# Pinning the issue order in the feed-forward part of a two-layer spectral and gated kernel

## The chip, the cores and the metric

The kernel runs on one core of a Trainium2 chip. The metric is the device time of one execution in microseconds (us). A core has five engines, each with a queue of its own: PE multiplies matrices (PEld is its weight load, which runs beside the matmuls), DVE (VectorE), ACT (ScalarE) and POOL (GpSimd) work element by element, and SP issues DMA transfers. They wait for one another by semaphores. PE writes into PSUM, which is divided into banks. A bank holds a 128x512 f32 tile here; POOL takes its operands from SBUF alone in this kernel.

## The reference

```python
x = A_x                                       # 1 x 2048 x 512, f32
for layer in range(2):
    n = layernorm(x)                          # over the 512 features, no weights
    x = x + irfft2(rfft2(n) * (w_r + 1j * w_i))       # over tokens and features
    n = layernorm(x)
    x = x + ((n @ w_gate) * (n @ w_up)) @ w_down      # 512 -> 1792 -> 512
...
```

The reference writes the two layers out one after the other; both use the same weights.

## The kernel before

**Stages.** `x` stays in SBUF as `xs`, 16 tiles of 128 tokens by 512 features. A layer is a spectral part and a feed-forward part. The spectral part is a forward transform of each tile (`fwd_steps`: tiles `fo`, `fe`, `tp`, `fs`, `dp`, `us`, `sp`, `E`), a middle phase (`mid_phase`) and an inverse transform of each tile (`inv_steps`: matmuls `vp`, ACT copies them to `vs[0]` and DVE makes the rest `vs[1]`, 12 matmuls `yi`, three DVE additions into `xs`, then the statistics of the next norm). The edges of the parts overlap with the feed-forward part by `weave`, which mixes a main list of steps with a side list by a cost written beside each step.

**Units.** The feed-forward part does the products by a 2x2 scheme with seven products instead of eight. `build_x` normalises two token tiles, transposes them on PE (`tq`) and makes the operand forms: `xA` (three blocks, ACT and DVE) and `xS` (four blocks of sums and differences: four POOL steps at lines 434 to 437, an ACT copy at line 440, a POOL subtraction at line 441). Every f32 operand is split in two, a rounded high part and a rest, and each product runs three matmuls (high by high, high by rest, rest by high; `mm3`, line 109), for two halves of the contraction: six matmuls a product.

`unit` does one of 14 blocks `ft` of 128 hidden features, gate and up, for two groups of 512 tokens (a full unit: eight tiles of `xs`) or two groups of 256 (half a unit: four tiles). For the first half of `xs` (`h0=0`) a layer runs four half units (blocks 0 and 1), ten full units (blocks 2 to 11) and four half units (blocks 12 and 13); for the second half (`h0=8`) it goes back through the blocks in reverse order: four half units, ten full ones, four half ones. Its steps are `p1` (PSUM tile `gx`), `p6` (`gy`), `p5` (`gw`), `p2` (into `gx` again), `p7` (`gz`), `p3` (`gv`), `p4` (into `gz` again). PSUM has one bank each for the tags x (`gx`), y (`gy`, `gz`) and w (`gw`, `gv`), three for tag a and two for tag d. ACT copies `gx` to `s1` (line 530); seven DVE steps (lines 536, 542, 551, 565, 566, 572, 573) add and multiply the products; the results are split into `h` by ACT (line 558) and POOL (line 559).

**Down products.** Each unit returns a list of down products, one for each 128 tokens of each of its two results (eight for a full unit, four for half a one), which the next unit mixes between its own products. A down product is three matmuls into a `db` bank (tag d) and a DVE addition into `xs` (line 580).

**Weights.** `load_raw` has SP fetch the raw weights of a block into `rg` (one buffer). `forms_w` makes the seven operand forms in `wt` (two buffers, even and odd blocks) from it: high parts `h...` on ACT (line 470), rests `l...` on POOL (line 473), differences `d...` in place on POOL (line 476). `down_w` does the same for the down weights (`rw`, `wd`, ACT line 491, POOL line 495). `beside` hands these steps out over the products of a unit, for the block after it (`eager` for a half unit).

**What sets the order.** The program is written in one sequence, but a scheduler decides the order in each engine's queue: it takes instructions by readiness in its own estimate and then by their written place, so an instruction that it takes to be ready may pass one that is written before it. On the chip every queue runs in the order that the scheduler left.

Of the kernel before, what the change touches and what calls it, by code (L numbers as in the profile page):

```python
# [13 lines left out]
EPS = 1e-5  # L14
# [73 lines left out]
def kernel(ctx: ExitStack, tc: tile.TileContext, x, wf, wc, wb, dfwd, dinv, tf, ti, mid, out):  # L88
# [18 lines left out]
    def mm3(o, sh, sl, mh, ml, start, stop):  # L107
        for n, (a, b) in enumerate(((sh, mh), (sh, ml), (sl, mh))):
            nc.tensor.matmul(o, a, b, start=start and n == 0, stop=stop and n == 2, skip_group_check=True)  # L109

    tt, stt = nc.vector.tensor_tensor, nc.vector.scalar_tensor_tensor
    gtt = nc.gpsimd.tensor_tensor
# [5 lines left out]
    nc.vector.memset(eps, EPS)  # L118
# [5 lines left out]
    def prep_hp(after):  # L124
        wct = wk.tile([128, 4, 2, 32], F32, name="wct", tag="tw", bufs=4)
        nc.gpsimd.tensor_copy(wct[0:1, 0, 0, 0:1], after)
        nc.sync.dma_start(wct, wc)
        for ri, col, src, op, scale in ((0, 0, 0, ALU.add, 0.5), (1, 0, 1, ALU.subtract, 0.5),
                                        (0, 1, 3, ALU.subtract, -0.5), (1, 1, 2, ALU.add, 0.5)):
            tt(hp[:, ri, :, col], wct[:, src, 0], wct[:, src, 1], op)  # L130
            nc.vector.tensor_scalar(hp[:, ri, :, col], hp[:, ri, :, col], scale, None, op0=ALU.mult)
# [19 lines left out]
    def stats(t, nm):  # L151
# [4 lines left out]
        nc.vector.bn_stats(st, xs[:, t])  # L156
        nc.vector.bn_aggr(nm["mv"][:, i], st)
# [7 lines left out]
    def rstd(nm):  # L165
# [4 lines left out]
        nc.scalar.activation(q, var, AF.Sqrt, bias=eps)  # L170
        small.extend([
            lambda: nc.vector.reciprocal(r0, q),
# [6 lines left out]
    def normed(t, nm):  # L179
        fill(9)  # L180
        xn = temp("xn", "g")
        i = nm["ts"].index(t)
        nc.vector.tensor_scalar(xn, xs[:, t], nm["mv"][:, i, 0:1], nm["r"][:, i:i + 1], op0=ALU.subtract, op1=ALU.mult)
        return xn
# [10 lines left out]
    def fwd_steps(get_dc, E, tags, gs, fs_dve):  # L195
# [4 lines left out]
        def a0(t):  # L200
# [4 lines left out]
            if i == 0:  # L205
                nc.vector.tensor_scalar(m2, nm["mv"][:, :n, 0], 2.0, None, op0=ALU.mult)
# [9 lines left out]
        def a1(t):  # L216
            s = S[t]
            tp = bank("tp", tags(t)[0])
            for i in range(4):
                src = s["fo"][:, i] if i < 2 else s["fe"][:, i - 2]  # L220
                nc.tensor.transpose(tp[:, 128 * i:128 * i + 128], src, ident)
            fs = s["fs"] = temp("fs", "f")
            if fs_dve(t):
                nc.vector.tensor_copy(fs, tp)
            else:
                nc.scalar.copy(fs, tp)

        def a2(t):
# [5 lines left out]
            for i, (n, c0) in enumerate(((256, 128), (256, 128), (128, 0), (128, 64))):  # L234
                mv = dc[:, o:o + n].rearrange("p (c k) -> p c k", c=2)
                nc.tensor.matmul(dv[:, :, c0:c0 + n // 2], fs[:, 128 * i:128 * i + 128], mv,  # L236
# [3 lines left out]
            nc.gpsimd.memset(u[64:128, :, 0:257:256], 0.0)  # L240
            i = nms[t]["ts"].index(t)
            r = nms[t]["r"][:, i:i + 1]
            for jj in range(2):
                q = slice(64 * jj, 64 * jj + 64)
                nc.scalar.mul(u[0:64, jj, 0:257], dp[q, 0:257], r[q])
                nc.scalar.mul(u[64:128, jj, 1:256], dp[q, 257:512], r[q])
                fill()

        def a3(t):
            s = S[t]  # L250
            tw, u = s["tw"], s["u"]
            for jj in range(2):
                sp = bank("sp", tags(t)[2])
                nc.tensor.matmul(sp[:, :257], tw[:, jj], u[:, jj, 0:257], start=True, stop=True)  # L254
                nc.scalar.copy(E[:, t, :, jj], sp[:, 0:257])
# [14 lines left out]
    class Filter:  # L270
# [5 lines left out]
        def load(self, n, after=None):  # L276
# [9 lines left out]
            if after is not None:  # L286
                nc.gpsimd.tensor_copy(self.at[n][0:1, 0, 0:1], after)
# [6 lines left out]
    def mid_phase(E, W):  # L294
# [3 lines left out]
        def turn(n, back):  # L298
            e = E[:, :, 16 * n:16 * n + 16].rearrange("p t k j -> p k t j")
            t = T[:, 16 * n:16 * n + 16].rearrange("p k (t j) -> p k t j", j=2)  # L300
            nc.vector.transpose(*((e, t) if back else (t, e)))

        def times_w(z, jz, w, p):
            nc.scalar.mul(jz[0:64], z[64:128], -1.0)
            nc.scalar.copy(jz[64:128], z[0:64])
# [3 lines left out]
        def spec(n):  # L309
            zp = bank("zp", XYW[n % 3])  # L310
            z = zp.rearrange("p (k g) -> p k g", g=32)
            nc.tensor.matmul(z, f2, T[:, 16 * n:16 * n + 16], start=True, stop=True)
# [15 lines left out]
        def unspec(n, y):  # L328
            yp = bank("yp", "a")
            y3 = yp.rearrange("p (k g) -> p k g", g=32)  # L330
            for i, m in enumerate(y):
                nc.tensor.matmul(y3, g2, m, start=i == 0, stop=i == len(y) - 1)
            nc.scalar.copy(T[:, 16 * n:16 * n + 16], y3)
# [5 lines left out]
        for i in range(20):  # L339
# [10 lines left out]
            if i == 0:  # L350
                nc.vector.transpose(tx[:, 0].rearrange("p (t j) -> p t j", j=2), E[:, :, 256])
                xp = bank("xp", "d")
                nc.tensor.matmul(xp[:, :32], f2, tx[:, 0], start=True, stop=True)
# [8 lines left out]
    def inv_steps(E, get_dc, nms, order, tags, build):  # L362
# [5 lines left out]
        def b1(t):  # L368
# [4 lines left out]
            for par in range(2):  # L373
                for jj in range(2):
                    nc.tensor.matmul(v4[:, par, :, jj], E[:, t, 128 * par:128 * par + 128, jj],
# [3 lines left out]
            nc.scalar.copy(vs[0], vp)  # L379
# [30 lines left out]
    def build_x(X, nm, tags):  # L410
# [9 lines left out]
        def turn(h):  # L420
            tq = bank("tq", tags[h])
            xn = s["xn"][h]
            for i in range(4):
                nc.tensor.transpose(tq[:, 128 * i:128 * i + 128], xn[:, 128 * i:128 * i + 128], ident)
            s[h] = tq.rearrange("p (b k s) -> p b k s", b=2, k=2)

        def forms():
            a, b = s[0], s[1]
            S = wk.tile([128, 4, 2, 128], F32, name="sx", tag="sx")
            nc.scalar.copy(S[:, 2:4], a)  # L430
            nc.scalar.copy(S[:, 0:2], b)
            nc.scalar.copy(XA[:, 0:2, 0, :, cols], a)
            nc.scalar.copy(XA[:, 2, 0, :, cols], b[:, 1])
# [313 lines left out]
```

## Time and profile before

| what | value |
|---|---|
| three runs | 1321.7, 1324.8, 1331.17 us; median 1324.8 us |
| the profiled execution's own time | 1329.39 us |
| its span, from the first to the last instruction | 1327.6 us |
| mean granted TensorE clock | 0.957 |
| layer 0, feed-forward part in the trace | about 142 to 696 us |
| layer 1, feed-forward part in the trace | about 790 to 1320 us |
| down products | 448, of three matmuls each |
| DVE waits for `db` on PE | 110.8 us in 151 waits |
| ACT waits for PE before the `wd` copy (line 491) | 199.8 us in 42 waits |

A profile is of one execution. A line names the place in the program, the engine and the tiles (out<-in). A wait is put down to what ended last before the waiting instruction began. A matmul's own duration overlaps with the next one's, so PE's pace is read from the starts. In the trace the start of line 572's addition marks the end of each unit: in layer 1 these lie at 801.9, 812.7, 831.6 and 839.5 us for the first four half units, at 858.6 to 1032.0 us for the ten full ones, at 1047.5 and 1055.2 us for the pair of half units after them, at 1063.6 to 1123.0 us for six more half units, at 1138.1, 1158.0, 1173.5 and so on to 1282.7 us for the ten full ones of the second half, and at 1295.5 to 1319.1 us for the last four.

### The profile page before, as it was taken

What the parts mean: (1) busy time and instruction counts of PE and PEld (TensorE: products, weight loads), DVE (VectorE), ACT (ScalarE), POOL (GpSimd) and SP (SyncE); (2) the same over time, 40 slices, a digit from 0 to 9 for tenths busy, and PEclk for the clock granted to TensorE, in tenths of its full rate; (3) what the DMA queues carried; (4) which work ended last, traced back from release to release, by engine and by line L of the source; (5) the groups of instructions that cost most, each with busy time, mean ns of one, the idle gap of its engine ahead of it and who ended that gap; (6) DMA issues with size and microseconds to landing.
All of it is one profiled execution on the core that took longest, in us unless ns stands there. A gap on an engine that the chain in (4) does not pass through costs nothing.

```text
span 1327.6 us, 16468 instructions
## 1 busy us (share of the span) xinstructions
PE 1188.2 (89%) x5804; PEld 958.1 (72%) x5804; DVE 896.1 (67%) x1669; ACT 460.9 (35%) x931; POOL 755.6 (57%) x788
## 2 busy tenths in 40 slices
PE   5888789989888889999998978999989878899998
PEld 4736678868667777788785467787776777677777
DVE  8578747768567866765685975586765655566666
ACT  5875323222222343344336732322212232322221
POOL 3543457565563676766622534766556465777772
PEclk9999889989999899999998988998999988999999
DMA  5541001112010011111105310111121021111111
GB/s 220 195 146 41 24 20 56 56 33 88 32 32 9 9 41 48 52 57 53 39 19 218 112 32 17 48 57 40 32 64 32 33 72 38 51 48 48 32 33 64
DMA packets 30754, 77.67 MB, mean 59 GB/s; under 512 B 3408, under 2 KB 11856, under 8 KB 28368
## 3 DMA queue, kind: packets, MB, share of 16 engines
q1 hardware_dynamic: 29952, 73.54, 16.8%
q0 software_dynamic: 288, 2.10, 0.5%
q8 instruction: 46, 0.75, 0.2%
q10 hardware_dynamic: 432, 0.98, 0.2%
q14 instruction: 36, 0.29, 0.1%
HBM read 72.42 MB, written 4.19 MB: 58 GB/s over the span
## 4 chain that ended last, share of the span: by engine, by line
PE 60%; POOL 20%; DVE 6%; issue 5%; ACT 5%; DMA 2%; POOLq 0%; ACTq 0%; SPq 0%; DVEq 0%
PE db L109 21%; PE gz L109 10%; PE gx L109 7%; POOL rg L476 5%; POOL wt L473 5%; PE gv L109 5%; PE gw L109 4%; POOL h L559 4%; PE gy L109 3%; PE yi L109 3%; PE dp L236 2%; PE sp L254 2%; POOL jz L307 2%; POOL xS L441 2%; DMA rg<-in_wb_dram 2%
## 5 line engine op out<-in xcount | busy, mean ns | idle before, releaser
L109 PE MATMUL db<-wd,h 128*128 128x512 f32 x1344 | 390.2, 412 | 56.1 <-POOL h L559 37.6
L580 DVE TENSOR_TENSOR xs<-xs,db 128x512 f32<-128x512 f32 x448 | 304.2, 684 | 112.2 <-PE db L109 110.8
L109 PEld LDWEIGHTS db<-wd,h 128*128 128x128 f32 x1344 | 246.9, 194 | 132.1 <-POOL h L559 56.5
L473 POOL TENSOR_TENSOR wt<-rg,wt 128x256 fp32r<-128x256 f32 x200 | 233.6, 1175 | 87.9 <-ACT wt L470 80.4
L470 ACT CAST wt<-rg 128x256 fp32r<-128x256 f32 x200 | 111.6, 567 | 335.6 <-POOL rg L476 209.5
L109 PE MATMUL gx<-xA,wt 128*128 128x512 f32 (+1 forms) x864 | 193.1, 359 | 7.3 <-DVE q L566 4.1
L559 POOL TENSOR_TENSOR h<-q,h 128x512 fp32r<-128x512 f32 (+1 forms) x144 | 151.5, 1057 | 82.8 <-ACT h L558 75.0
L495 POOL TENSOR_TENSOR wd<-rw,wd 128x512 fp32r<-128x512 f32 x52 | 67.2, 1294 | 196.0 <-ACT wd L491 176.9
L109 PEld LDWEIGHTS gx<-xA,wt 128*128 128x128 f32 x864 | 148.2, 199 | 36.9 <-DVE q L566 8.7
L476 POOL TENSOR_TENSOR rg<-rg 128x256 f32<-128x256 f32 x200 | 158.7, 794 | 8.1
L536 DVE TENSOR_TENSOR q<-gy,s 128x512 f32<-128x512 f32 (+1 forms) x72 | 41.2, 572 | 134.5 <-ACT s L530 61.5
L109 PE MATMUL gy<-xS,wt 128*128 128x512 f32 (+1 forms) x432 | 98.9, 362 | 23.8 <-ACT xS L440 15.7
L109 PE MATMUL gw<-xS,wt 128*128 128x512 f32 (+1 forms) x432 | 105.8, 368 | 0.1
L109 PEld LDWEIGHTS gy<-xS,wt 128*128 128x128 f32 x432 | 74.2, 200 | 38.5 <-ACT xS L440 17.4
L491 ACT CAST wd<-rw 128x512 fp32r<-128x512 f32 x52 | 32.1, 620 | 199.9 <-PE db L109 199.8
L558 ACT CAST h<-q 128x512 fp32r<-128x512 f32 (+1 forms) x144 | 74.6, 523 | 68.4 <-DVE q L566 57.1
L109 PE MATMUL gv<-xS,wt 128*128 128x512 f32 (+1 forms) x432 | 97.4, 348 | 0.0
L109 PE MATMUL gz<-xS,wt 128*128 128x512 f32 (+1 forms) x432 | 91.8, 350 | 0.0
L109 PE MATMUL gz<-xA,wt 128*128 128x512 f32 (+1 forms) x432 | 90.7, 346 | 0.0
L109 PEld LDWEIGHTS gw<-xS,wt 128*128 128x128 f32 x432 | 77.9, 206 | 10.4 <-issue 0.4
L109 PEld LDWEIGHTS gv<-xS,wt 128*128 128x128 f32 x432 | 73.9, 194 | 12.2
L109 PEld LDWEIGHTS gz<-xS,wt 128*128 128x128 f32 x432 | 74.3, 197 | 11.5
(99 smaller groups left out, 1649.2 us busy)
## 6 DMA issues: line engine op xcount, KB each, us to landing
rg<-in_wb_dram SPq DMA_DIRECT2D x50, 512.0 KB, 3.6
rw<-in_wb_dram SPq DMA_DIRECT2D x52, 256.0 KB, 2.6
wq<-in_wf_dram SPq DMA_DIRECT2D x10, 1024.0 KB, 5.4
wr<-in_wf_dram SPq DMA_DIRECT2D x6, 1024.0 KB, 5.3
tw<-in_tf_dram SPq DMA_DIRECT2D x32, 128.0 KB, 2.8
tw<-in_ti_dram SPq DMA_DIRECT2D x32, 128.0 KB, 2.1
out_dram<-xs SPq DMA_DIRECT2D x16, 256.0 KB, 2.0
xs<-in_x_dram SPq DMA_DIRECT2D x7, 512.0 KB, 7.9
```

The costliest lines, as they stand in the source:

```text
L109: nc.tensor.matmul(o, a, b, start=start and n == 0, stop=stop and n == 2, skip_group_check=True)
L236: nc.tensor.matmul(dv[:, :, c0:c0 + n // 2], fs[:, 128 * i:128 * i + 128], mv, start=i == 0, stop=i == 3, skip_group_check=True)
L254: nc.tensor.matmul(sp[:, :257], tw[:, jj], u[:, jj, 0:257], start=True, stop=True)
L470: nc.scalar.copy(box["w"][:, 0, o:o + n], box["r"][:, r:r + n])
L473: gtt(box["w"][:, 1, o:o + n], box["r"][:, r:r + n], f32(box["w"][:, 0, o:o + n]), ALU.subtract)
L476: gtt(box["r"][:, o], box["r"][:, a], box["r"][:, b], ALU.subtract)
L491: nc.scalar.copy(wds["t"][:, ft % 2, 0], box["r"])
L495: gtt(w[:, 1], box["r"], f32(w[:, 0]), ALU.subtract)
L536: tt(q, y[:, :n], box["s1"], ALU.add)
L558: nc.scalar.copy(t[:, 0], h)
L559: gtt(t[:, 1], h, f32(t[:, 0]), ALU.subtract)
L580: tt(xs[:, t], xs[:, t], dp, ALU.add)
```

## The change

Three things are changed together.

1. The calls on DVE, ACT, POOL and PE go through a small class that, between two places in the program, ties each instruction behind the one written before it on its engine. The scheduler can then no longer reorder these four engines in the feed-forward parts of both layers and what is woven into them. The spectral part in between and the transfers that SP issues are not tied.
2. The products of a unit come in the order p5, p1, p6, p2, p7, p3, p4. The addition of `gw` moves from p5 to p6, behind that of `gy`. The down products of the unit before come later: none after the first three products, three of eight after p2, the other five after p7.
3. The weight steps are handed out anew, with finer steps in the eager list; side steps are not woven in behind p3 and p4 (`hold`); two weaves use up their side list by 0.7 of the main one.

```diff
+    pin = {"on": False}
+    class Queue:
...
+        def __getattr__(self, name):
+            f = getattr(self.engine, name)
+            def call(*args, **kw):
+                ins = f(*args, **kw)
+                if pin["on"]:
+                    tc.keep_in_program_order(ins)
+                return ins
+            return call
+    V, A, G, TE = (Queue(e) for e in (nc.vector, nc.scalar, nc.gpsimd, nc.tensor))
...
-        names = ("start dstart h0 h1 l0 d0", "l1 d1 d2", "d3 h3 h5", "l5", "l3 next", "dh", "dl") if eager else \
-            ("start dstart h0 h1", "l0 d0", "l1 d1", "d2 d3", "h3 h5 dh dl", "l3", "l5 next")
+        names = ("start dstart", "h0 h12 l0 d0 h3 l3", "d1 l12 d2", "h5 l5 h4", "l4 d3 h6 l6 next", "dh", "dl") \
+            if eager else ("start dstart", "h0 h12 l0 d0", "l12 d1", "d2 d3 h34", "h56 l34 l56 next dh dl", "", "")
...
         def p6():
...
             q = box["q"] = new("q")
+            q5 = box["q5"] = new("q5")
             tt(q, y[:, :n], box["s1"], ALU.add)
+            tt(q5, box["w"][:, :n], q, ALU.add)
 
         def p5():
-            w = bank("gw", "w")
-            prod(w, 4, 3, True, True)
-            q5 = box["q5"] = new("q5")
-            tt(q5, w[:, :n], box["q"], ALU.add)
+            box["w"] = bank("gw", "w")
+            prod(box["w"], 4, 3, True, True)
...
-        for i, p in enumerate((p1, p6, p5, p2, p7, p3, p4)):
-            ops.append((c, p))
-            upto = len(prev) * (0, 1, 3, 5, 8, 8, 8)[i] // 8
+        for i, p in enumerate((p5, p1, p6, p2, p7, p3, p4)):
+            ops.append((c, p) if i < 5 else ("hold", c, p))
+            upto = len(prev) * (0, 0, 0, 3, 8, 8, 8)[i] // 8
...
-            while side and (s + side[0][-2] * 0.5) / st <= m / mt:
+            while o[0] != "hold" and side and (s + side[0][-2] * 0.5) / st <= m / mt:
...
+        pin["on"] = True
         weave(units([(0, 0), (1, 0)], 0), rest)
...
-        weave(units([(12, 1), (13, 1)], 0), b1)
-        weave(units([(13, 0), (12, 0)], 8), b2)
+        weave(units([(12, 1), (13, 1)], 0), b1, 0.7)
+        weave(units([(13, 0), (12, 0)], 8), b2, 0.7)
...
+            pin["on"] = False
             emit(in_steps([o for o in fb if o[0] >= K] + fc))
```

In the new lists `h12` and `l12` are the old `h1` and `l1` (two blocks in one step), `h34`, `l34`, `h56`, `l56` are the old `h3`, `l3`, `h5`, `l5`, and a name with one digit does one block.

## The prediction

> **What bounds the kernel now.** I read the page's busy table first, then who waited for whom on PE, then the busy time by stage, then the chain of waits inside one bad place and the timeline of one good place.
>
> ```profile
> PE 1188.2 (89%) x5804; PEld 958.1 (72%) x5804; DVE 896.1 (67%) x1669; ACT 460.9 (35%) x931; POOL 755.6 (57%) x788
> ```
> ```profile
> PE db L109 <- POOL h L559: 37.6, 24, 3.1
> PE gy L109 <- ACT xS L440: 15.7, 8, 2.2
> PE db L109 <- ACT h L558: 14.9, 9, 2.5
> PE gy L109 <- POOL xS L441: 8.1, 8, 1.3
> ```
> PE is the bound, and what holds it in the feed-forward part is late `h` (52.5 us) and late `xS` (23.8 us). The busy time by stage, layer 1 (columns: us, length, then PE, PEld, DVE, ACT, POOL busy, granted clock, DMA share, GB/s):
>
> ```profile
> 790.00:839.50 49.50, 41.08 (x249) 37.79 (x248) 29.35 (x68) 13.86 (x31) 26.10 (x28) 0.86 0.04 11
> 839.50:1032.00 192.50, 177.71 (x808) 142.96 (x807) 128.06 (x216) 49.65 (x95) 117.14 (x114) 0.96 0.16 47
> 1032.00:1123.00 91.00, 77.42 (x471) 68.35 (x471) 54.42 (x106) 24.93 (x53) 49.10 (x52) 0.92 0.13 44
> 1123.00:1283.00 160.00, 154.37 (x652) 121.13 (x652) 103.24 (x148) 44.04 (x82) 116.08 (x113) 0.99 0.15 48
> ```
> The last row is nearly full; the idle time is in the three before it. Layer 0 looks the same. Why `h` is late, from the chain of waits:
>
> ```profile
> 1031.41 0.42 ACT wt L470
> 1031.83 0.07 issue
> 1031.90 0.75 POOL wt L473
> 1032.64 0.07 issue
> 1032.71 1.24 POOL rg L476
> 1033.95 1.22 POOL wt L473
> 1035.18 0.68 POOL rg L476
> 1035.86 1.24 POOL h L559
> 1037.10 0.04 issue
> 1037.14 1.19 PE db L109 x4
> ```
> The scheduler put four weight operations of the next tile ahead of the `h` that PE needed: 3.06 us of PE lost here. And the quiet place, where the price list comes from:
>
> ```profile
> 1194.14 1.54 PE L109 MATMUL db<-wd,h 128*128 128x512 f32 x6
> 1195.52 1.52 PE L109 MATMUL gx<-xA,wt 128*128 128x512 f32 x6
> 1196.88 1.52 PE L109 MATMUL db<-wd,h 128*128 128x512 f32 x6
> ```
> ```profile
> 1184.88 1.37 DVE L580 TENSOR_TENSOR xs<-xs,db 128x512 f32<-128x512 f32 x2
> 1185.62 0.53 PEld L109 LDWEIGHTS db<-wd,h 128*128 128x128 f32 x3 [0.30 <-DVE xs L580]
> 1185.63 0.97 PE L109 MATMUL db<-wd,h 128*128 128x512 f32 x3
> ```
> Six matmuls start every 1.36 us (0.227 each), so a full unit (7 products of 6, 8 down products of 3) needs 14.96 us of PE; half a unit 7.5. The line-572 additions, one a unit, start 15.60 us apart here, so 0.64 is stall. A DVE addition takes 0.69 and starts 0.21 after its matmuls; a freed bank is used 0.05 later with 0.11 of weight load showing, together 0.16.
>
> **The change, part by part.**
>
> Pinning adds no instruction. The finer weight steps add 16 on ACT and on POOL, 0.26 us each on POOL (two of 0.78 for one of 1.30), 4 us over the run beside PE: nothing, unless POOL is late in those eight half units, and then 0.5 us in each. SP's transfers are not pinned and stand in nearly the same order; `rg` is asked for after the last reader, 11.6 us into a unit, takes 3.6, and is read at 18.8: free, with 3 us to spare. PE's product order hardly changes: the built program of before already runs gw, gx, gy. What moves are the down products (first one at 5.4 us into a unit, not 4.1 or earlier), `h` (now ahead of the next tile's weights on ACT and POOL), and everything that the scheduler used to slip into a stall.
>
> Quiet full unit, walked through its new PE order (gw gx gy gx, 3 downs, gz, 5 downs, gv, gz): the four products end at 5.44; two downs fill the two `db` banks, the third waits for the first's addition (6.33 to 7.02) and ends at 7.86 instead of 7.48; gz ends at 9.22; its addition occupies DVE to 10.12, so the fourth and fifth downs' additions end at 10.81 and 11.50; the sixth down ends 0.39 late, the eighth 0.37. The unit lasts 16.1 us, 0.5 more than now. `h` is ready 2.1 us (first half) and 3.9 us into the unit, on POOL 1.30 each after c12 and c21: not late any more. POOL's weights then run to 11.6 us, `dl` to 15.1: 11.4 us of work in 16, no bound.
>
> Units with an inverse tile (PE 1.9 more: vp 0.47, yi 12 x 0.118). DVE gets vs[1] (0.69, behind a 0.6 ACT copy), three xs additions (1.5) and stats (0.85), in written order between the `db` additions. Where vs[1] stands before the fourth down's addition, the walk gives 19.0 us (2.1 stall); where it stands in front of the third's, 17.75 (0.9 stall). Ten units: seven with eight tiles are 7 x 14.96 + 15.2 - 2.7 (the first has four downs only) = 117.2 plus 8 x 0.9 to 8 x 2.1, three quiet ones 48.3: 173 to 182 against 192.5. I take 180, nearer the worse walk, since DVE also shares time with POOL (the 573 product takes 1.09 instead of 0.69): **-12 a layer**.
>
> First four half units. Now gx runs while `xS` is made, and four downs and a yi fill the wait before the second pair of columns. Then gw, which reads `xS`, comes first and holds all that is behind it, and the last yi comes after gz of the second unit: it ends about 810.5 instead of 808.5 us. From there to `xS` is 16.4 us now (808.5 to 824.9), and 18.0 with the two `h` ahead on POOL: 828.5, with four downs and gx (3.4 us) still to do. The third half unit ends about 836.5 instead of 831.6: **+5 a layer**, between 0 (if yi is not later) and +8.
>
> The pair of units after the ten: the first has eight downs, 4.8 + 5.4 + 1.2 of bank stalls = 11.4 against 15.6, because the chain above is gone; the second 7.9 against 7.6: **-3.5 a layer** (down to -1 if POOL's eager weights, 8.2 us in an 11.4 us unit, hold its `h`).
>
> The six half units with the token pairs: now 70.0 us (layer 0) and 67.8. The side work ends at 0.7 of the weave and not behind the last two products. From the last tq, two S copies (1.2), four POOL steps (3.3), xS on ACT (1.05) and on POOL (2.4) are 8.0 us; the rest of the unit is 5.8. So gw waits 2.5 to 3 us at two places where 13.8 to 14.6 us units stand now; one `h` behind xS on POOL costs 1.6. Unit by unit 8.7, 9.9, 11.5, 10.2, 11, 8: about 60: **-10 and -8**, between -3 and -12.
>
> Ten units of the second half: layer 1 12.6 + 9 x 16.1 = 157.5 against 159.7: **-2** (the two 20 us starts are gone, the quiet ones cost more). Layer 0 with eight forward tiles of 1.52: 169.7 plus a stall of 1 us a tile, as their DVE steps are as long as a vs[1]: 178 against 175: **+3**, between -5 and +10. Last half units: -1 each layer. Spectral parts: not pinned, the same order: 0.
>
> Sum: layer 0 5 - 12 - 3.5 - 10 + 3 - 1 = -18.5, layer 1 5 - 12 - 3.5 - 8 - 2 - 1 = -21.5; together -40. The profiled execution took 1329.4 (span 1327.6), which gives 1289; it lay 4.6 above the median of the three runs, 1324.8, and on that scale the time is **1285 us**.
>
> **Rivals.**
>
> *Half the gain.* POOL stays the releaser of the downs, since in written order `h` stands behind the eager weights and behind xS. Where it does, the pair, the six half units and the first unit after each lose about 20 of their 27 us (7 and 18, and 2 at the starts): 1305 us. For it: the six half units' walk has it once. Chance 0.10.
>
> *Nothing moves.* The product order was already there, and quiet units are near 14.96 anyway; what is saved at `h` returns at the `db` banks, gw and tq, and only the pairs of units keep their gain (-7), less some quiet units' 0.5: 1320. For it: DVE's wait for `db` is 110.8 us, so PE leads DVE by little. Against: the 52.5 us have a cause that pinning removes. 0.13.
>
> *Slower, by DVE's head.* A pinned DVE instruction that waits for ACT holds all additions behind it, and with two `db` banks PE stops after two downs. Price: ACT stands 199.8 us in 42 waits for `wd`, 4.8 each; a vs or fs copy queued behind such a wait costs 3.6 us more than my 1.2. 24 tiles make 86, so 1371 us. It decides the sign from 40 / 24 = 1.7 us a tile, over 1% from 2.2. For it: DVE waited 7.3 us for such a copy at the longest now. Against: in the units that I walked the copy stands ahead of `wd`. 0.12.
>
> *Slower, by the clock.* Where PE stalls often the granted clock is low: 0.86 in the first stage above, 0.99 in the last. Three short stalls in each of 40 full units could take these from about 0.97 to 0.86: 40 x 14.96 x (1/0.86 - 1/0.97) = 79 us, so 1364. Against it: 840 to 1032 has 15 us of idle time and still 0.96. 0.04. The Trainium skill ("TensorE: Matmul & The Clock Gate", A second HAM failure mode: psum-queue depth-cycling) describes this: cycling through PSUM banks idles PE briefly between groups and the clock swings between half and full. By that rule at its worst such units would run at half clock; the row of the last stage, with a bank stall in every unit, does not show it.
>
> **How the numbers follow.** The forecast has 0.61. A measurement of this kernel tells about 1% (13 us) from no change, so faster means under 1311.6 and slower over 1338. Faster: 0.61 + 0.10 = 0.71; same: 0.13; slower: 0.12 + 0.04 = 0.16. Low end: the better walk of the ten units (-19), and +0 in the first stage (-10), are 29; not both in full, so 1260. High end: through the half case to 1320, where nothing moves. This leaves out the slower cases and a little below, 0.2.
>
> **What would show it.** Right: the `h` steps (558, 559) follow line 573 without a 470 or 473 between, PE's wait for `h` falls from 52 us to under 15, full quiet units are 16.1 apart, the ten units take 173 to 182, and a new wait of gw for `xS` appears with 8 us before the third half unit of a layer. Wrong: quiet units over 17 us, PE's wait for DVE xs (2.4 us now) above 60, or a granted clock under 0.95 between 1145 and 1280.

## The result and the profile after

| kernel | median (runs) | profiled: span | mean clock |
|---|---|---|---|
| before | 1324.98 us (4) | 1327.6 us | 0.957 |
| changed | 1368.22 us (4; 1365.74 to 1371.37) | 1369.6 us | 0.956 |

The changed kernel takes 1.0322 times as long, interval [1.0279, 1.0365]. The forecast of 1285 us had the wrong sign, and the range ends below the result.

The busy table and the chain's shares, from the page of the changed kernel:

```profile
PE 1199.9 (88%) x5804; PEld 945.9 (69%) x5804; DVE 901.1 (66%) x1669; ACT 468.4 (34%) x947; POOL 765.3 (56%) x804
...
PE 53%; DVE 22%; POOL 12%; issue 7%; ACT 4%; DMA 1%; POOLq 0%; SPq 0%; DVEq 0%; ACTq 0%
```

The work is the same, yet DVE now ends 22% of the chain (6% before). Who PE waited for in the changed kernel (total us, times, longest); in this trace every step carries the line of the wrapper's call, L123, so tiles tell them apart:

```profile
PE db L123 <- DVE xs L123: 30.9, 27, 3.7
PE tq L123 <- DVE xn L123: 22.9, 8, 4.1
PE gw L123 <- ACT xS L123: 22.3, 4, 6.1
PE tp L123 <- POOL fo L123: 17.5, 6, 5.8
```

PE's wait for `h`, 52.5 us before, is 0.9 us:

```profile
PE db L123 <- ACT h L123: 0.7, 1, 0.7
PE db L123 <- POOL h L123: 0.2, 1, 0.2
```

That wait was cured. The four others have grown in its place: before, they were 2.4 us (`db` for `xs`), 11.0 (`tq` for `xn`), 15.7 (`gy`, then the first product to read `xS`, for ACT's part of it) and 9.6 (`tp` for `fo`). The same four stretches of layer 1 as in the prediction, in the changed kernel (us, length, then PE, PEld, DVE, ACT, POOL busy, granted clock, DMA share, GB/s):

```profile
831.00:896.50 65.50, 44.48 (x254) 40.05 (x255) 30.51 (x68) 13.95 (x30) 25.06 (x28) 0.79 0.04 11
896.50:1081.00 184.50, 174.51 (x811) 137.94 (x810) 121.57 (x195) 50.40 (x95) 118.91 (x115) 1.00 0.15 49
1081.00:1164.50 83.50, 74.22 (x478) 63.93 (x477) 63.42 (x125) 25.80 (x56) 49.92 (x54) 1.00 0.14 48
1164.50:1323.50 159.00, 155.82 (x650) 118.61 (x649) 100.12 (x146) 45.46 (x83) 118.72 (x115) 1.00 0.15 49
```

Three of the four are shorter, as forecast; the first is 16 us longer at a clock of 0.79. By stage, from the first `tq` and the starts of the addition that ends a unit:

| stage | before | after | difference | forecast |
|---|---|---|---|---|
| first four half units, layer 0 / 1 | 63.0 / 63.0 | 78.9 / 78.9 | +15.8 / +15.9 | +5 each |
| ten units with inverse tiles | 192.6 / 192.5 | 184.7 / 184.7 | -7.8 each | -12 each |
| pair of half units | 23.2 / 23.2 | 20.7 / 20.7 | -2.5 each | -3.5 each |
| six half units | 70.0 / 67.8 | 62.7 / 62.7 | -7.3 / -5.1 | -10 / -8 |
| ten units, second half, layer 0 (forward tiles) | 174.9 | 207.4 | **+32.5** | +3 |
| ten units, second half, layer 1 | 159.8 | 159.2 | -0.5 | -2 |
| last four half units | 44.5 / 36.4 | 49.8 / 37.2 | +5.3 / +0.8 | -1 each |
| spectral parts and the end | 216.9 | 222.1 | +5.3 | 0 |

They add to the 42.0 us between the two spans, but for rounding. Two stages carry it: the first four half units, twice, and the forward stretch of layer 0.

One border moved with the change. In the kernel before, the scheduler had put the statistics of all eight forward tiles and the steps `fo`, `fe` and `tp` of two to three of them into the six half units ahead of the forward stretch; in the changed kernel all of this work lies in the stretch. So part of the +32.5 and of layer 0's -7.3 is work that changed places: the two stages together take 244.9 us before and 270.0 after, +25.2.

The start of the first, layer 1, in the timeline of PE of the changed kernel (start, duration, tiles, count; in brackets the idle time before it and what ended that):

```profile
827.92 1.94 PE L123 MATMUL tq<-midt,xn 128*128 128x128 f32 x8 [4.08 <-DVE xn L123]
834.88 0.58 PE L123 MATMUL gw<-xS,wt 128*128 128x256 f32 x1 [5.02 <-ACT xS L123]
837.30 1.43 PE L123 MATMUL gw<-xS,wt 128*128 128x256 f32 x5 [1.84 <-POOL xS L123]
838.53 1.48 PE L123 MATMUL gx<-xA,wt 128*128 128x256 f32 x6
839.81 1.89 PE L123 MATMUL vp<-tw,E 128*128 128x128 f32 x8
...
846.45 1.58 PE L123 MATMUL yi<-di,vs 128*128 128x256 f32 x12
```

`gw` reads `xS`, the last form to be made, and is now the first product of the unit. Pinned, it stands at the head of PE's queue for 6.86 us, with `gx` (which needs only `xA`), a `vp` and two tiles' `yi` behind it. (A `yi` of one tile is 12 matmuls.) The last matmul of the last `yi` but one starts 30.4 us after the first `tq`; before it was 15.2. The second pair of columns, and a second wait of `gw`, follow later by as much. Behind such waits the matmuls also run slower: half a unit's products start 1.28 us apart (838.53, 839.81), 0.72 where PE is not held.

The forward stretch in the timelines of PE, DVE and POOL of the changed kernel:

```profile
485.42 0.69 PE L123 MATMUL tp<-midt,fo 128*128 128x128 f32 x2 [5.76 <-POOL fo L123]
485.90 0.64 PE L123 MATMUL tp<-midt,fe 128*128 128x128 f32 x2
486.19 2.91 PE L123 MATMUL gx<-xA,wt 128*128 128x512 f32 x6
...
492.62 0.85 PE L123 MATMUL db<-wd,h 128*128 128x512 f32 x3
...
499.22 0.98 PE L123 MATMUL db<-wd,h 128*128 128x512 f32 x3 [3.70 <-DVE xs L123]
```
```profile
492.39 0.78 DVE L123 TENSOR_SCALAR rs<-mv 128x2 f32<-128x2 f32 x1
493.28 0.83 DVE L123 SCALAR_TENSOR_TENSOR fo<-xs,rs 128x256 f32<-128x256 f32 x1
494.15 1.46 DVE L123 TENSOR_TENSOR fe<-fo 128x128 f32<-128x128 f32 x2
495.53 0.15 DVE L123 RECIPROCAL rs<-rs 128x2 f32<-128x2 f32 x1
495.72 0.56 DVE L123 SCALAR_TENSOR_TENSOR rs<-mv,rs 128x2 f32<-128x2 f32 x1
496.31 1.46 DVE L123 SCALAR_TENSOR_TENSOR rs<-rs 128x2 f32<-128x2 f32 x2
497.70 0.68 DVE L123 BATCH_NORM_STATS2 st<-xs 128x6 f32<-128x512 f32 x1
498.41 0.18 DVE L123 BATCH_NORM_AGGREGATE mv<-st 128x2 f32<-128x6 f32 x1
498.51 0.65 DVE L123 TENSOR_TENSOR xs<-xs,db 128x512 f32<-128x512 f32 x1
```
```profile
483.38 1.30 POOL L123 TENSOR_TENSOR wd<-rw,wd 128x512 fp32r<-128x512 f32 x1
484.65 1.40 POOL L123 TENSOR_TENSOR fo<-xs 128x256 f32<-128x256 f32 x2
```

The first `db` product ended about 493.3 us; its addition starts at 498.51. DVE went through 6.1 us of small steps of a forward tile (from 492.39) first, so with two banks the third down product waits 3.70 us. And the transposes `tp` of a forward tile hold PE 5.76 us for a `fo` that POOL starts only at 484.65, behind the pinned weight steps, two `h` and a `wd`.

### The profile page after: what moved, and what is told of

It is laid out like the page before. It is cut to its first block, busy times and chain, and to the rows that moved or that the text cites. A ratio compares the mean times of both kernels' runs of the same rounds, so it can differ in the third digit from the quotient of the medians.

```text
span 1369.6 us, 16523 instructions
## 1 busy us (share of the span) xinstructions
PE 1199.9 (88%) x5804; PEld 945.9 (69%) x5804; DVE 901.1 (66%) x1669; ACT 468.4 (34%) x947; POOL 765.3 (56%) x804
## 3 DMA queue, kind: packets, MB, share of 16 engines
q1 hardware_dynamic: 29952, 73.54, 15.8%
## 4 chain that ended last, share of the span: by engine, by line
PE 53%; DVE 22%; POOL 12%; issue 7%; ACT 4%; DMA 1%; POOLq 0%; SPq 0%; DVEq 0%; ACTq 0%
PE db L123 13%; DVE xs L123 10%; PE gx L123 9%; PE gz L123 8%; PE gw L123 4%; PE gy L123 4%; PE gv L123 4%; DVE q L123 3%; PE yi L123 3%; POOL wt L123 3%; PE dp L123 2%; POOL jz L123 2%; PE sp L123 2%; DVE st L123 2%; PE vp L123 2%
## 5 line engine op out<-in xcount | busy, mean ns | idle before, releaser
L123 PE MATMUL db<-wd,h 128*128 128x512 f32 x1344 | 378.1, 408 | 42.1 <-DVE xs L123 30.9
L123 DVE TENSOR_TENSOR xs<-xs,db 128x512 f32<-128x512 f32 x448 | 304.2, 685 | 106.6 <-PE db L123 105.9
L123 PEld LDWEIGHTS db<-wd,h 128*128 128x128 f32 x1344 | 235.2, 189 | 141.5 <-DVE xs L123 101.9
L123 POOL TENSOR_TENSOR wt<-rg,wt 128x512 fp32r<-128x512 f32 (+1 forms) x216 | 232.8, 1085 | 135.7 <-ACT wt L123 134.8
L123 POOL TENSOR_TENSOR h<-q,h 128x512 fp32r<-128x512 f32 (+1 forms) x144 | 167.9, 1185 | 167.5 <-ACT h L123 167.5
L123 PE MATMUL gx<-xA,wt 128*128 128x512 f32 (+1 forms) x864 | 189.2, 356 | 5.8 <-ACT s L123 5.6
L123 ACT CAST wt<-rg 128x512 fp32r<-128x512 f32 (+1 forms) x216 | 110.6, 539 | 183.3 <-POOL rg L123 168.4
L123 PEld LDWEIGHTS gx<-xA,wt 128*128 128x128 f32 x864 | 144.2, 197 | 28.5 <-ACT s L123 10.5
L123 ACT CAST h<-q 128x512 fp32r<-128x512 f32 (+1 forms) x144 | 75.6, 525 | 233.5 <-DVE q L123 232.6
L123 POOL TENSOR_TENSOR rg<-rg 128x256 f32<-128x256 f32 x200 | 147.6, 738 | 10.7
L123 PE MATMUL gw<-xS,wt 128*128 128x512 f32 (+1 forms) x432 | 97.6, 359 | 43.3 <-ACT xS L123 22.3
L123 DVE TENSOR_TENSOR q<-gy,s 128x512 f32<-128x512 f32 (+1 forms) x72 | 41.2, 572 | 139.9 <-PE gy L123 55.9
L123 POOL TENSOR_TENSOR wd<-rw,wd 128x512 fp32r<-128x512 f32 x52 | 69.0, 1328 | 85.7 <-ACT wd L123 85.7
L123 PEld LDWEIGHTS gw<-xS,wt 128*128 128x128 f32 x432 | 72.1, 195 | 60.4 <-ACT xS L123 23.9
L123 PE MATMUL gy<-xS,wt 128*128 128x512 f32 (+1 forms) x432 | 93.9, 355 | 0.0
L123 POOL TENSOR_TENSOR sx<-sx 128x256 f32<-128x256 f32 x64 | 47.7, 745 | 78.9 <-ACT sx L123 75.1
L123 PE MATMUL gz<-xS,wt 128*128 128x512 f32 (+1 forms) x432 | 90.8, 346 | 0.6 <-DVE q L123 0.6
L123 PE MATMUL gv<-xS,wt 128*128 128x512 f32 (+1 forms) x432 | 91.2, 347 | 0.0
L123 PE MATMUL gz<-xA,wt 128*128 128x512 f32 (+1 forms) x432 | 90.4, 346 | 0.0
L123 PEld LDWEIGHTS gz<-xS,wt 128*128 128x128 f32 x432 | 72.8, 190 | 13.9 <-DVE q L123 1.0
L123 PEld LDWEIGHTS gv<-xS,wt 128*128 128x128 f32 x432 | 72.9, 192 | 12.8
L123 PEld LDWEIGHTS gy<-xS,wt 128*128 128x128 f32 x432 | 73.0, 199 | 9.3
```

Source lines behind the costliest of these rows:

```text
L123: ins = f(*args, **kw)
```

## The experiments

An expectation names its theories by letters; what matters of each is said in words behind it. Stage times are compared with 78.9 (first four half units), 184.7 (ten with inverse tiles), 207.4 (forward stretch) and 16.17 us (a quiet full unit) of the changed kernel. All ratios are to the kernel before, run beside it.

### Which part of the change: the pin or the order

**The kernel before with the pin alone**, between the same two places:

```diff
+        pin["on"] = True
         weave(units([(0, 0), (1, 0)], 0), rest)
...
+            pin["on"] = False
             emit(in_steps([o for o in fb if o[0] >= K] + fc))
```

> The kernel before with the pin alone, in the same stretches; product order, down products and weight steps as before. Theory A (the pin costs in the two weaves, the new order is made to suit a pinned queue): slower than before by 30 us or more, 1355 to 1420 us, with the first weave and the forward weave long. Rival (the new order costs): within 15 us of before, 1310 to 1340 us.

1608.8 us, ratio 1.2118 [1.2076, 1.216], clock 0.891: slower, as expected, but by far more. A quiet unit takes 22.16 us on average. Its longest wait on PE (total, times, longest):

```profile
PE gy L123 <- POOL wt L123: 157.9, 40, 5.2
```

The old places of the weight steps work only because the scheduler moves them.

**The changed kernel, never pinned:**

```diff
-        pin["on"] = True
         weave(units([(0, 0), (1, 0)], 0), rest)
```

> The changed kernel with the pin never on: the scheduler decides, from the new written order. Theory A: both weaves are short again, the quiet units keep the price of the later down products (16.0 to 16.3 us instead of 15.6) unless the scheduler moves them, 1310 to 1345 us. Rival (the new order costs): 1350 us or more.

1424.2 us, 1.0732 [1.0686, 1.0779], on the rival's side; a quiet unit 17.27 us. PE's longest wait here:

```profile
PE gx L123 <- ACT s L123: 123.1, 45, 9.2
```

With the new order and no pin, `p2` waits for the ACT copy `s1`, 45 times. So each half of the change alone is harmful, +21% and +7%; together they are +3%. The parts can't be priced one by one and added. Of the new order, only the places of the down products were tried by themselves (below); those of the products and of the weight steps were not.

**The pin on only after the first weave of each layer:**

```diff
-        pin["on"] = True
         weave(units([(0, 0), (1, 0)], 0), rest)
+        pin["on"] = True
```

> The changed kernel with the pin switched on only after the first weave of each layer (the four first half units with the rest of the inverse transform). Theory A, the pin costs there because PE stands behind tq and gw while the chain from yi to xS runs: the first weave gets back most of what it lost, 10 to 19 us a layer, so 1331 to 1348 us, and the third and fourth half units of layer 1 end about 13 us earlier against the ends of layer 0. Rival, the new product order (gw, which needs xS, first) and the later down products cost it, whoever decides the order: under 5 us a layer come back, 1358 to 1368 us.

1347.3 us, 1.0145 [1.0106, 1.0184]. The first four half units take 68.9 and 68.4 us: of the 16 us a layer, 10 are the pin's in this weave. About 5.5 remain. The third and the fourth half unit are still pinned in this run, and the wait of `gw` before the third one is still there, 6.87 us in layer 1:

```profile
852.74 0.58 PE L123 MATMUL gw<-xS,wt 128*128 128x256 f32 x1 [5.03 <-ACT xS L123]
855.16 1.44 PE L123 MATMUL gw<-xS,wt 128*128 128x256 f32 x5 [1.84 <-POOL xS L123]
```

In the kernel that is never pinned the same `gw` waits 1.01 and 1.34 us in layer 1, and the four half units take 64.5 and 63.2 us, nearly the 63.0 of before. So most of the rest is the pin's too. (Part of it moves on there: the first full unit behind takes 23.8 and 24.7 us in that kernel, 19.0 and 19.1 before.)

**The pin off in layer 0 from the forward stretch on:**

```diff
         if layer == 0:
+            pin["on"] = False
             dcs["f"] = load_df()
```

> The changed kernel with the pin off in layer 0 from the weave of the second ten full units with the forward transform on. Theory A, DVE in written order works on forward steps while finished down products wait for it and PE fills its two db banks: the ten units take about 175 to 182 us instead of 207 and the last half units 45 instead of 50, so 1330 to 1345 us. Rival, the later down products cost it by themselves: the ten units stay over 195 us, over 1355 us.

1365.8 us, 1.0292 [1.0256, 1.0328]; the stretch takes 206.4 us, on the rival's side: taking the pin off as such does not give the 32.5 us back. But the wait is another one, as the weight loads show, first the changed kernel between 478 and 735 us, then this one:

```profile
PEld db L123 <- DVE xs L123: 28.0, 32, 4.1
```
```profile
PEld gx L123 <- ACT s L123: 28.8, 10, 5.8
```

The scheduler pays with the `s1` wait seen above what it saves on DVE, so this run could not tell whether DVE's written order costs anything. One engine at a time had to be freed.

### The forward stretch: DVE, POOL and the banks

**DVE alone left to the scheduler there**, and then **DVE and POOL** (the second tests `not in` a pair, `(nc.vector, nc.gpsimd)`):

```diff
-                if pin["on"]:
+                if pin["on"] and self.engine is not pin["free"]:
                     tc.keep_in_program_order(ins)
...
         if layer == 0:
+            pin["free"] = nc.vector
             dcs["f"] = load_df()
```

> The changed kernel with DVE alone left to the scheduler in layer 0 from the weave of the second ten full units with the forward transform to the end of the layer; PE, ACT and POOL stay pinned there. Theory B, the loss there is DVE doing forward steps in written order while the db additions behind them hold PE's two banks: PE's wait for DVE xs in that stretch (28 us at the weight loads) falls by half or more and the ten units take 180 to 192 us instead of 207, 1343 to 1357 us. Rival, any pinned queue does it (POOL and ACT): no change above 5 us.

1355.4 us, 1.0199 [1.0153, 1.0246]; 193.6 us for the stretch, 13.8 less, a little short of what was expected. The wait of `db` for DVE falls from 28.0 to 17.1 us, not by half:

```profile
PEld db L123 <- DVE xs L123: 17.1, 30, 1.8
```

> As the kernel with DVE alone free in layer 0 from the forward weave on, with POOL free there too; PE and ACT pinned. Theory B with POOL's part: the first unit of the weave waits 6 us for the forward step fo, which POOL has behind the eager weight steps, h and dl; with POOL free it falls from 23.5 to about 17 us and the ten units to about 185, 1345 to 1350 us. Rival, the wait at the entry is on DVE's side or on the transform's own chain: the first unit stays over 22 us.

1350.3 us, 1.0172 [1.0134, 1.021]; 187.9 us, 5.7 less again. The first unit takes 17.4 us (28.8 in the changed kernel, 23.5 with DVE free); the second becomes 4.1 us longer, and the rest 3.8 shorter together. The transposes that waited 5.76 us for `fo` wait no more, and `gx` behind them is back to its pace (start to start 1.47 us):

```profile
480.25 1.63 PE L123 MATMUL gw<-xS,wt 128*128 128x512 f32 x6
481.71 0.38 PE L123 MATMUL tp<-midt,fo 128*128 128x128 f32 x2
481.93 0.38 PE L123 MATMUL tp<-midt,fe 128*128 128x128 f32 x2
482.07 1.64 PE L123 MATMUL gx<-xA,wt 128*128 128x512 f32 x6
```

**A third bank for `db`** in the changed kernel, taken from tag a:

```diff
-    NB = {"x": 1, "y": 1, "w": 1, "a": 3, "d": 2}
+    NB = {"x": 1, "y": 1, "w": 1, "a": 2, "d": 3}
```

> The changed kernel with three PSUM banks for the down products and two instead of three for tag a. Theory C, a quiet unit's 16.17 us is 14.96 of PE plus the third, sixth and eighth down product waiting for a bank: with a third bank the quiet units take 15.1 to 15.5 us, some 26 us over all quiet units if tag a does not miss its bank; 1335 to 1350 us. Rival, the 1.2 us are waits for h, s1 or weights: quiet units stay within 0.2 of 16.17.

1315.2 us, 0.9895 [0.9858, 0.9932], better than expected. Only the six half units become longer, 66.1 and 65.8 us (62.7 in the changed kernel); in layer 1 their granted clock is 0.92 in place of 1.00. A quiet unit takes 14.96 us, the price list's sum without a stall, the ten units with inverse tiles 172.7 (12.0 less), the forward stretch 194.7 (12.7 less). The five down products in a row of one quiet unit, in the changed kernel and with three banks:

```profile
1219.40 4.34 PE L123 MATMUL db<-wd,h 128*128 128x512 f32 x15
1223.58 1.55 PE L123 MATMUL gv<-xS,wt 128*128 128x512 f32 x6
```
```profile
1175.77 3.56 PE L123 MATMUL db<-wd,h 128*128 128x512 f32 x15
1179.17 1.07 PE L123 MATMUL gv<-xS,wt 128*128 128x512 f32 x4
```

4.18 us from start to start against 3.40.

**The same bank in the kernel before:**

> The kernel before with three banks for the down products and two for tag a. Theory C says that before interleaves its down products so that a bank is missed only once in a quiet unit (0.12 us of the 0.64 stall): quiet units stay at 15.4 to 15.6 us and the time within 1% of before, 1312 to 1335 us. Rival, the banks were short in before too: under 1305 us.

1294.0 us, 0.9765 [0.9732, 0.9797]: below what was expected. A quiet unit gains only 0.2 us (15.39), but the ten units with inverse or forward tiles gain 7.9, 7.5 and 2.9 us, the first four half units 4.2 and 5.8, and the spectral parts with the end 5.4. In the kernel before, too, two banks were a limit wherever DVE has side work, as the rival said. It also means that with three banks in both, the change still loses (0.9895 against 0.9765).

**All three for the forward stretch together:** DVE and POOL free there, and three banks.

> DVE and POOL left to the scheduler in the forward stretch of layer 0, and tags a:2, d:3 instead of a:3, d:2. In the forward stretch the ten full units took 207.4 us in the changed kernel, 187.9 with DVE and POOL free, 194.7 with the third db bank. If the two gains are separate waits they add: 175 us, the same as before the change (174.9), and 1295 to 1300 us. If they are partly the same wait, counted twice: 180 to 188 us, 1300 to 1310 us, and the forward stretch would keep a cost that neither names.

1295.8 us, 0.9777 [0.9729, 0.9825]; the stretch takes 175.5 us (175 if the gains are separate waits). So the 32.5 us are DVE's written order (13.8), POOL's (5.7) and the bank waits that are left then (12.4), freed in this order (POOL alone was not tried); 0.6 remains. The freed engines take some of the tiles' work (the statistics of all eight, `fo` of one or two) back into the six half units before, which take 65.4, 65.9 and 67.9 us in these three runs. Over both stages the shares are 11.1, 5.1 and 10.5 us: from 270.0 to 243.4, where the kernel before takes 244.9. And the third bank helps that kernel too, by 2.9 us in this stretch (to 172.0).

**Down products spaced out.** Two behind each of `p2`, `p7`, `p3` and `p4`:

```diff
-            upto = len(prev) * (0, 0, 0, 3, 8, 8, 8)[i] // 8
+            upto = len(prev) * (0, 0, 0, 2, 4, 6, 8)[i] // 8
```

with `dh dl` behind the last of them.

> The changed kernel with the eight down products two behind each of p2, p7, p3 and p4 (in place of three behind p2 and five behind p7), and the down weights' steps dh and dl moved behind the last of them. Theory C: no down product finds its bank taken, quiet units take 15.0 to 15.4 us, the woven ones gain as much or more, 1320 to 1340 us. Rival as for the three banks: quiet units within 0.2 of 16.17 us.

1509.3 us, 1.136 [1.1318, 1.1403]. In this kernel the two down products of a full unit behind `p4` take the `h` of the unit just computed, since `p4` has replaced the buffer that they should read. So it computes something else than the reference. Its longest wait on PE is `db` for ACT's `h` (101.8 us in 40 waits), and it says nothing on the banks. **Two behind each of `p6`, `p2`, `p7` and `p3`** keep clear of that:

```diff
-            upto = len(prev) * (0, 0, 0, 3, 8, 8, 8)[i] // 8
+            upto = len(prev) * (0, 0, 2, 4, 6, 8, 8)[i] // 8
```

> The changed kernel, two banks as it has, with the eight down products two behind each of p6, p2, p7 and p3 (not three behind p2 and five behind p7), and dh and dl behind the last. Theory C, it is runs of more than two that wait: quiet units 14.96 to 15.3 us, the woven ten units shorter by 5 us or more a layer, 1318 to 1345 us. Rival, DVE is late for the banks whatever the spacing: quiet units over 15.9 us.

1305.5 us, 0.9844 [0.9813, 0.9875], below what was expected: a quiet unit 14.98 us with two banks, the ten units with inverse tiles 170.4, the forward stretch 193.7. No run of more than two downs, no wait in a quiet unit: the 1.2 us that the changed kernel pays in each come from its runs of three and five. In the forward stretch, too, the spacing (13.6 us) is worth as much as the third bank (12.7).

### The first weave: whose order

**PE alone left to the scheduler in the first weave of each layer**, and **DVE alone** (`nc.vector` in its place):

```diff
-        pin["on"] = True
+        pin["on"], pin["free"] = True, (nc.tensor,)
         weave(units([(0, 0), (1, 0)], 0), rest)
+        pin["free"] = ()
```

> The changed kernel with PE alone left to the scheduler while the first two half units of each layer are woven with the side list; DVE, ACT and POOL stay pinned there. The first four half units took 78.9 us a layer with the pin and 68.9 and 68.4 with all four engines free. Theory P: it is PE's own written order that costs the 10 us (tq and gw wait at the head of PE's queue in front of down products that could run): 68 to 72 us a layer, 1347 to 1355 us. Theory D: it is DVE's written order (xn behind other DVE steps): 76 to 79 us a layer here, 1362 to 1369 us, and the 10 us come back in the run with DVE free.

1352.0 us, 1.0204 [1.016, 1.0248]; 69.9 and 71.5 us for the first four half units, as theory P expected: 9.0 and 7.3 of the 10 us come back. PE's timeline of this run at the place shown above:

```profile
819.82 1.63 PE L123 MATMUL yi<-di,vs 128*128 128x256 f32 x6
821.33 0.58 PE L123 MATMUL gx<-xA,wt 128*128 128x256 f32 x1
821.71 0.84 PE L123 MATMUL yi<-di,vs 128*128 128x256 f32 x5
822.39 0.76 PE L123 MATMUL gx<-xA,wt 128*128 128x256 f32 x5
822.99 0.28 PE L123 MATMUL yi<-di,vs 128*128 128x256 f32 x1
825.22 0.52 PE L123 MATMUL gw<-xS,wt 128*128 128x256 f32 x1 [1.95 <-ACT xS L123]
```

A `yi` and `gx` fill the wait, and `gw` waits 1.95 us, not 5.02.

> The changed kernel with DVE alone left to the scheduler in the first weave of each layer; PE, ACT and POOL stay pinned there. Theory P (PE's order costs it): 76 to 79 us for the first four half units, 1362 to 1369 us. Theory D (DVE's order costs it): 68 to 72 us a layer, 1347 to 1355 us. If neither run comes below 74 us, it takes several engines together, and the cause is not one queue.

1359.1 us, 1.0254 [1.0212, 1.0296]; 74.3 and 73.1 us, between the two forecasts: 4.6 and 5.8 us. The two gains add to more than the 10 us, so they are partly the same wait. A chain in which the two queues hold each other (`yi` on PE, statistics and `xn` on DVE, `tq` on PE) would explain that; it was not tried apart. PE's is the larger part.

### What can be had

**Old order without pin where the change lost, new order with pin elsewhere** (old: first four half units of each layer, and layer 0 from the forward stretch on):

```diff
-        for i, p in enumerate((p5, p1, p6, p2, p7, p3, p4)):
-            ops.append((c, p) if i < 5 else ("hold", c, p))
-            upto = len(prev) * (0, 0, 0, 3, 8, 8, 8)[i] // 8
+        for i, p in enumerate((p1, p6, p5, p2, p7, p3, p4) if old else (p5, p1, p6, p2, p7, p3, p4)):
+            ops.append((c, p) if i < 5 or old else ("hold", c, p))
+            upto = len(prev) * ((0, 1, 3, 5, 8, 8, 8) if old else (0, 0, 0, 3, 8, 8, 8))[i] // 8
...
```

> The order and freedom of before in the places where the change lost (the first four half units of each layer; in layer 0 all units from the weave with the forward transform on), the changed order with the pin in the rest. Theory: the gains of the rest stand alone, -7.8 twice for the ten units, -2.5 twice, -7 and -5 for the six half units, 28 to 33 us under before, 1292 to 1300 us. Rival, the gains there depend on what went before them (work that the late places had pushed on): over 1312 us.

1301.8 us, 0.9798 [0.9764, 0.9832], a little above what was expected. The ten units with inverse tiles (183.6 and 183.7) and the pairs keep their gain, and the lost stages are back at 59.5, 60.7 and 178.6 us. The six half units keep part of it in layer 1 (64.2), but not in layer 0 (69.8): there the scheduler again has the first steps of the forward tiles in them. With **three banks**, and then with **two downs behind each of `p6`, `p2`, `p7`, `p3`** in its new-order units as well:

> The hybrid (order and freedom of before in the first four half units and in layer 0 from the forward weave on, the changed order and the pin elsewhere) with three PSUM banks for the down products and two for tag a. Theory C: the pinned full units fall from 16.13 to 14.96 us and the woven ten units by 11 us a layer, as with three banks alone, 1262 to 1280 us. Rival, the free stretches need the third bank of tag a: they get longer by what the others gain, over 1290 us.

1249.7 us, 0.9423 [0.9397, 0.945], clock 0.983, below what was expected.

> The mixed kernel with the third db bank, and in its new-order units two down products each behind p6, p2, p7 and p3 instead of three and five. If the third bank and the spacing cure the same wait, nothing is left: 1247 to 1252 us. If spacing gives more, for the late h or the units with inverse tiles: 1238 to 1246 us.

1239.8 us, 0.9357 [0.9316, 0.9398], the fastest of the study. The spacing takes another 4.4 us from each layer's ten units with inverse tiles (171.2 to 166.8) and nothing to quiet units (14.96 both): with three banks, runs of five are short of banks only beside DVE's side work. One such run took 3.79 us in the kernel of 1249.7 us (from 823.24) where 3.40 is its time without a wait; the rest of the 4.4 us was not taken apart. Of the page of the fastest kernel:

```profile
PE 1140.7 (92%) x5804; PEld 937.1 (76%) x5804; DVE 891.3 (72%) x1669; ACT 462.2 (37%) x941; POOL 760.2 (62%) x798
...
PE 69%; POOL 12%; DVE 8%; ACT 6%; issue 5%; DMA 1%; POOLq 0%; SPq 0%; ACTq 0%; DVEq 0%
```

PE has 69% of the chain, 60% in the kernel before, and the clock is 0.984.

## Why the prediction was wrong

**Right.** The late `h` was the cause of PE's waits, and the change removes it (52.5 us to 0.9). The walk of the quiet unit gave 16.1 us; it is 16.17. The stages that only the pin, the late downs and `h` decide went the forecast way at 64 to 73% of the forecast size: ten units with inverse tiles 184.7 us (173 to 182 forecast), pairs -2.5, six half units -7.3 and -5.1. The new wait of `gw` for `xS` before the third half unit is there, forecast as 8 us, measured 7.96 (6.12 for ACT's part and 1.84 for POOL's).

**The step that failed most: "178 against 175: +3" for the forward stretch**, with "a stall of 1 us a tile, as their DVE steps are as long as a vs[1]". A `vs[1]` is one step of 0.69 us. The forward steps in front of one addition are ten instructions and 6.1 us in the timeline above. The stretch took 207.4 us where the sum had 178; the term was +32.5, 4.1 us a tile. Its parts are shown by runs: DVE's order 13.8, POOL's 5.7, banks 12.4. The 175 it was set against is itself too low a base, since the scheduler had part of the tiles' work in front of the stretch: with the six half units counted in, the loss is 25.2 us and the forecast was -7. That POOL's `fo` would stand behind weight steps was not in the walk: of the moved steps, only `h` was followed on POOL.

**The second: +5 for the first four half units** (measured +15.8 and +15.9). The walk put the wait of `gw` for `xS` before the third half unit and held the last `yi` to be 2 us later. The same wait stands before the first half unit already (6.86 us), with `yi` behind it: the last `yi` but one is 15 us later and the last 9 (31.8 to 41.0 us after the first `tq`). Freeing PE's queue alone in the first weave gives 9.0 and 7.3 us back, freeing all four engines there 9.9 and 10.5. The third half unit then ends 5.6 and 5.1 us later than before, counted from the first `tq`, behind the wait that the walk named (6.87 us in layer 1). So the +5 itself was near, and what the walk left out is the pin's cost in the first weave, about 10 us a layer. And the walk used full-speed products behind the stalls. At 1.28 instead of 0.72 us, the 3.8 products from 877.40 to 882.47 us alone cost 2.3 us.

**The small terms.** Last four half units of layer 0: +5.3 for -1. With the pin off from the forward stretch on they take 44.2 us, the old time, so this too is the pin. The spectral parts and the end, forecast 0, are +5.3; no run took this apart, but where the stretches beside them have the old order and no pin (1301.8 us) they take 217.7 us, 0.9 over the kernel before.

**The rivals.** *Slower, by DVE's head* named 1371 us, and 1368.2 came. It is half right: additions are held behind pinned DVE steps until two banks are full, in the forward tiles. But there DVE does not wait for an ACT copy behind `wd`, as the rival had it; it is busy with the tile's own steps (492.39 to 498.51). Its order and the banks come to 26.2 us in eight tiles, 3.3 a tile where the rival priced 3.6. And it charged all 24 tiles: the 16 inverse ones made their stage shorter, and what it left out, PE's own head in the first weave, made up for them. So the time was right by luck, by errors that cancel; chance 0.12 was too low for the eight tiles whose DVE steps the trace of before had and that I did not add up. *Half the gain* and *nothing moves* fell with `h`: the gain was there in its stages and was lost in others. *Slower, by the clock*: quiet units run at a granted clock of 1.00 with a bank stall in each. The low clock stands around waits of several us: 0.79 from 831 to 896.5 us. After PE has waited 6.12 and 1.84 us, products take 1.28 us at a granted clock of 0.50, and after 5.1 us of work 0.72 at 1.00. From 864.8 to 868.8 us it is 0.58 as well, behind waits of 1.73 and 2.12 us with a down product between them. The Trainium skill ("TensorE: Matmul & The Clock Gate", What's actually happening) states half rate after an idle window of about 3.4 us, and full rate after a busy one of that length. The half rate agrees, and the return took 5.1 us here. In this case the clock is thus a multiplier on long stalls, not a cause of its own.

**The signs.** Of the signs of being wrong (quiet units over 17 us, PE's wait for DVE's `xs` above 60, a clock under 0.95 between 1145 and 1280 us) none came: 16.17, 30.9 and 1.00. All three looked for trouble in the steady units or over the whole run, and the loss was at the edges.

## What to carry to other kernels

Before an order is pinned, walk every queue at every edge where other work is woven in, not only the steady unit: for each instruction that waits, list what is queued behind it and could have run, and sum all the small steps in front of an addition that frees a bank. A pinned order and the order that a scheduler leaves are different starting points, and one written for the one is bad under the other (here +21% and +7%), so pin by engine and by stage and keep the parts that gain. Short accumulations that are followed by an addition want one more bank (three were enough here for a run of five where DVE had no other work), or to be spaced so that none waits.

## What was unexpected in the hardware

One more `db` bank is worth 2.3% on the kernel before and, on the changed one, 3.9% of its time (1368.2 to 1315.2 us), far more than the 0.6 us of stall in a quiet unit of the kernel before, and 1.1 in one of the changed kernel, of which the prediction knew. After the waits of 6.86 and 7.96 us PE runs at half rate for 4 to 5 us (granted clock 0.50 from 837.3 to 841.4 and from 877.4 to 882.5 us).

And DVE's small steps are long beside POOL. Two engines in the timeline of the forward stretch of the changed kernel:

```profile
496.50 1.26 POOL L123 TENSOR_TENSOR wt<-rg,wt 128x512 fp32r<-128x512 f32 x1
496.51 1.27 DVE L123 SCALAR_TENSOR_TENSOR rs<-rs 128x2 f32<-128x2 f32 x1
```

A step on two numbers a partition takes 1.27 us, as long as the POOL instruction that began just before it; the same step takes 0.16 us where POOL rests (two in 0.36 us at 850.77). Over the whole trace, the 43 `rs` steps of this form that no POOL instruction overlaps take 0.12 to 0.16 us; of the 25 that one overlaps, 12 take 0.65 to 2.18. The Trainium skill ("SBUF — State Buffer", SBUF: two separate sides) says that a DVE instruction with two SBUF inputs and a GpSimd one take turns at a shared pair of ports, each for the whole instruction. The pair of lines agrees. So a small DVE step with two such inputs in a pinned queue must be priced with the POOL instruction that it may fall beside.
